# Attention and two feed-forward stages on one core: the products with v in four visits a pair instead of six, a later turn of the last rows, and weight conversions behind the exp

## The chip, the cores and the metric

One NeuronCore of a Trainium2 chip runs the whole kernel. The metric is the device time of one execution in microseconds. The kernel before took 1120.94 us in the median of three runs (1120.7 to 1121.53).

## What is computed

Rotary attention over 4 sequences of 576 positions with 8 heads of 64, then two feed-forward layers over the 2304 tokens. All is float32.

```python
def _attn_ref(q, k, v):                      # (4, 8, 576, 64)
    q_rot, k_rot = rotate(q), rotate(k)      # x1*cos - x2*sin, x1*sin + x2*cos
    scores = 1/sqrt(D) * q_rot @ k_rot.T
    attn = exp(scores - max(scores))
    attn = attn / (sum(attn) + 1e-9)
    return attn @ v
x = attention output as (2304, 512)
x = (h - tanh(h)) @ w_out,   h = x @ w_in        # 512 -> 2048 -> 512
x = (h * sigmoid(h)) @ w_out, h = x @ w_in
```

## The kernel before

The attention stage fills the first 320 us, the two feed-forward layers the rest. The program's order is written out by hand: each engine runs its instructions in the order in which the code issues them.

Attention goes by **pairs** of heads of one sequence: 16 pairs (`NP`), numbered from 0. A pair has 9 row tiles (`tiles`): 4 full tiles of 128 rows for each of the two heads, alternating, and one tile of the remaining 64 rows of both. The loop over `g` makes one **step** for each tile, 144 in all; `n` is the step within the pair, 0 to 8. Every step does this, in this order:

- `scores(g)`: TensorE multiplies a tile of q with the high and the low part of k (`kh`, `kl`) into one of two PSUM score buffers `sc`. Full precision is had by splitting numbers into a high and a low part.
- `rest(g - 2)` transposes the last columns of the p tile of two steps earlier into the score buffer of this step (steps 0, 1, 3, 5 and 7); `row_max(g)` on VectorE; `qk_low` makes low parts on VectorE; `transposes(g - 2)` turns four 128-blocks of p on TensorE (`tpp`), ScalarE copies them out to `pt`, and VectorE copies the last columns to `pr`.
- rotation of the next pair's q and k (`rope_upto`, `rope_dup` and two or one pieces from the list `rq`), on GpSimd.
- `recip_spread` (steps 4 and 7): the reciprocals of the row sums, made by GpSimd into `rw`, are turned on TensorE (`tpb`), and ScalarE copies them to `rs`.
- `pv`: products with v of the pair before. A pair has 20 (`NPV`), each two passes on TensorE, 10 into a wide half of 320 columns and then 10 into a narrow half of 256. A run of them in one step is called a **visit**; the table `PV_N` says how many there are in which step. Its index is `n2`, which is the step less 2 (modulo 9). When a half is complete, `x_out` multiplies it with `rs` on VectorE and SP stores it to `xd`.
- `conv.run`: conversions of weights for the feed-forward layers, a number of pieces by the table `CONV_RATE`. A weight tile takes four VectorE instructions, on ScalarE a Square (`wm`) and a copy (`w`), and on GpSimd a subtraction (`w`).
- `qk_high` (steps in `QK_AT`): TensorE turns the rotated q or k of the next pair (`tpq`), four blocks of 128 for q and each k, two for the remaining rows (`ar`); ScalarE copies out the high part (`qs`, `kh`, `qr`). The low part comes from `qk_low` a step later.
- `exps(g)`: exp on ScalarE into `p`. The scores of step g + 2 use the same score buffer, and its transposes need this p.

In step 2 SP issues the loads of v, in step 5 the loads of the next but one pair's q and k (`load_qk`, into `xm` and `xr`).

Of the kernel before, what the change touches and what calls it, by code (L numbers as in the profile page):

```python
# [29 lines left out]
def kernel(  # L30
# [26 lines left out]
    TW = [MAIN] * B + [B * REM]  # L57
    NH = NF // 2

    CONV_RATE = (1.6, 0.0, 0.0, 0.0, 0.0, 0.0, 0.0, 1.5, 1.5)  # L60
    RATE_0 = 0.01
    SPLIT_AT = 2

# [266 lines left out]
    TPB = 3  # L330
    NPV = 4 * (NJ + 1)
    Q0 = 256
    QK_AT = {1: 0, 3: 1, 5: 2, 6: 3}
    ON_DVE = ((1, 1),)
    R_AT = (4, 7)
    PV_N = (4, 0, 4, 2, 0, 4, 0, 4, 2)

    def attention(conv, on_rope_done, on_scores_near, on_scores_done):
        es_main, es_even, es_odd, es_rope, es_sc = (ExitStack() for _ in range(5))
# [18 lines left out]
        def load_qk(i):  # L358
            b, c = divmod(i, NPAIR)
            hs = slice(2 * c, 2 * c + 2)  # L360
            xm = [rp.tile([128, 2, NJ * D], F32, tag=f"xm{n}", name=f"xm{n}", bufs=1) for n in range(2)]
            xr = rp.tile([128, 2, D], F32, tag="xr", name="xr", bufs=1)
            for n, src in ((1, k), (0, q)):
                nc.sync.dma_start(
                    out=xm[n],
                    in_=src[b, hs, 0:MAIN, :].rearrange("h (p j) d -> p h (j d)", j=NJ),
                )
            if i == 0:
                nc.sync.dma_start(out=csr, in_=cs_rem)
            for n, src in ((0, q), (1, k)):  # L370
                nc.sync.dma_start(
                    out=xr[64 * n:64 * n + 64, :, :],
                    in_=src[b, hs, MAIN:S, :].rearrange("h p d -> p h d"),
                )
            raw_t[i] = (xm, xr)

        def load_v(i):
            b, c = divmod(i, NPAIR)
            vm = ap.tile([128, 2, NJ, D], F32, tag="vm", name="vm", bufs=2)

            vr = vr2[i % 2]
            nc.sync.dma_start(
                out=vm.rearrange("p h j d -> p h (j d)"),
                in_=v[b, 2 * c:2 * c + 2, 0:MAIN, :].rearrange("h (p j) d -> p h (j d)", j=NJ),
            )
            for h in range(2):
                nc.sync.dma_start(out=vr[64 * h:64 * h + 64, h], in_=v[b, 2 * c + h, MAIN:S, :])
            v_t[i] = (vm, vr)
# [40 lines left out]
        def rope_dup(i, u):  # L429
            if u > 0:  # L430
                a = rot_t[i][u]
                if i:
                    POOL.tensor_copy(out=a[:, :, 1, :], in_=a[:, :, 0, :])
                else:
                    ACT.activation(out=a[:, :, 1, :], in_=a[:, :, 0, :], func=ACTF.Copy)

        def qk_alloc(i):
            qk_t[i] = [qkp[i % 2].tile([128, 2 * S + (REM if nm != "qs" else 0)], F32R, tag=nm, name=nm, bufs=1)
                       for nm in ("qs", "kh", "kl")]
            qk_t[i].append(qr2[i % 2])  # L440
# [3 lines left out]
        KO = (0, 2 * S - MAIN)  # L444
        up, dn = slice(0, 64), slice(64, 128)

        def qk_high(i, u):
            src = rot_t[i][u]
            qs, kh, kl, qr = qk_t[i]
            tp = ps.tile([128, 512], F32, tag="tp", name="tpq", bufs=TPB)  # L450
            for j in range(NJ if u < 3 else 2):
                PE.transpose(tp[:, j * 128:(j + 1) * 128], src[:, j].rearrange("p e d -> p (e d)"), ident)  # L452
            if u == 0:
                parts = [(qs[up, 0:MAIN], tp[up], qs[dn, 0:MAIN]), (qs[dn, S:S + MAIN], tp[dn], qs[up, S:S + MAIN])]
            elif u < 3:
                parts = [(kh[:, KM[u - 1]], tp, kl[:, KM[u - 1]])]
            else:
                t4 = tp[:, 0:256].rearrange("p (h s) -> p h s", h=2)
                parts = [(qr[up, h, h * 64:h * 64 + 64], t4[up, h, 0:64], qr[dn, h, h * 64:h * 64 + 64])
                         for h in range(2)]  # L460
                kc = slice(MAIN, MAIN + 128)
                parts.append((kh[:, kc].rearrange("p (h s) -> p h s", h=2), t4[:, :, 64:128],
                              kl[:, kc].rearrange("p (h s) -> p h s", h=2)))
                parts.append((kh[:, 2 * S:], t4[:, 1, 64:128], kl[:, 2 * S:]))
            for hi, t, lo in parts:
                ACT.activation(out=hi, in_=t, func=ACTF.Copy)  # L466
            return parts

        def qk_low(parts):
            for hi, t, lo in parts:  # L470
                DVE.tensor_tensor(out=lo, in0=t, in1=hi.bitcast(F32), op=ALU.subtract)  # L471
# [23 lines left out]
        def row_max(g):  # L495
            st = ap.tile([128, 1], F32, tag="st", name="st", bufs=4)
            DVE.tensor_reduce(out=st, in_=s_t[g][:, :, 0:HALF], op=ALU.max, axis=AX.XY, negate=True)  # L497
            st_t[g] = st

        def exps(g):  # L500
            i, n = divmod(g, NTI)
            if n == 0:
                sum_t[i] = ap.tile([128, NTI], F32, tag="sums", name="sums", bufs=2)
            sc, st = s_t.pop(g), st_t.pop(g)
            h = tiles[n][0]
            if h != 1:
                p_t[g] = ap.tile([128, 2, S], F32, tag="p", name="p", bufs=2)
            else:
                p_t[g] = p_t[g - 1]
            p = p_t[g][:, h % 2]  # L510
            ACT.activation(out=p.rearrange("p (e s) -> p e s", e=2), in_=sc[:, :, 0:HALF],  # L511
                           func=ACTF.Exp, bias=st, accum_out=sum_t[i][:, n:n + 1])
# [111 lines left out]
        def rope_push(i):  # L624
            for n in range(5):
                rq.extend((i, n, f) for f in rope_ops(i, n, DVE if (i, n) in ON_DVE else POOL))

        def rope_upto(i, n):
            while rq and rq[0][:2] <= (i, n):
                rq.pop(0)[2]()  # L630
# [28 lines left out]
        parts = []  # L659
# [6 lines left out]
        while True:  # L666
            i, n = divmod(g, NTI)
            more = i + 1 < NP
            if 0 < i < NP and n == 2:
                load_v(i)  # L670
            if i + 2 < NP and n == 5:
                rope_upto(i + 1, 4)
                load_qk(i + 2)
                rope_push(i + 2)
            d = g - LAG - NTI
            i2, n2 = divmod(d, NTI)

            live = g < G

            if live:  # L680
                scores(g)
                if more and n == 0:
                    qk_alloc(i + 1)
                if g == 0:
                    parts.extend(first[2:5] + first[6:] + qk_high(0, 2))
            if 0 <= g - LAG < G:
                rest(g - LAG, g)
            if live:
                row_max(g)
            qk_low(parts)  # L690
            parts.clear()
            if 0 <= g - LAG < G:
                transposes(g - LAG)

            if more and QK_AT.get(n) == 0:
                rope_upto(i + 1, 1)
            elif more and n + 1 in QK_AT:
                rope_upto(i + 1, QK_AT[n + 1] + 1)
                rope_dup(i + 1, QK_AT[n + 1])
            if live:  # L700
                for _ in range(2 if n % 3 else 1):
                    if rq:
                        rq.pop(0)[2]()

            if 0 < i <= NP:
                at = R_AT if i < NP else (2, 2)
                if n == 0:
                    recips(i - 1)
                for e in (1, 0):
                    if n == at[1 - e]:  # L710
                        recip_spread(i - 1, e)
            if d >= 0:
                if n2 == 0:
                    pvq.extend((i2, m) for m in range(NPV))
                for _ in range(PV_N[n2] if live else NPV // 2):
                    if pvq:
                        pv(*pvq.pop(0))
            rate = (CONV_RATE[n] if i else RATE_0) / 2 if live else 0.0
            conv.run(rate)
            if more and n in QK_AT:  # L720
                parts.extend(qk_high(i + 1, QK_AT[n]))
            if live:
                exps(g)
            conv.run(rate)
            if g == G - NTI:
                es_rope.close()
                es_even.close()
                on_rope_done()
            if g == G - SPLIT_AT:
                on_scores_near()  # L730
            if g == G - 1:
                es_odd.close()
                es_sc.close()
                on_scores_done()
            if g >= G:
                on_tail(g - G)
            if d > 0 and i2 == NP - 1 and not pvq:
                break
            g += 1
# [234 lines left out]
    conv = Conv()  # L974
# [250 lines left out]
```

## Time and profile before

| | before |
|---|---|
| median of three runs | 1120.94 us |
| profiled execution | 1120.96 us |
| its span | 1119.2 us |
| TensorE busy | 1095.6 us (98%) |
| VectorE busy | 852.4 us (76%) |
| ScalarE busy | 681.6 us (61%) |
| GpSimd busy | 255.3 us (23%) |

The span is the time from the first to the last instruction of the program; the profiled execution's own time is 1.8 us longer. A busy TensorE isn't TensorE at its peak: matmuls are pipelined, and the ends of the records are modelled, so two records may overlap. What a piece of work costs is read from its start to the start of the next piece. GpSimd's work lies nearly all in the attention stage.

### The profile page before, as it was taken

Reading aid. Unit: us, or ns where it says so; the run is one execution under the profiler, and the core shown is the slowest. Engines: PE = TensorE matmul, PEld = TensorE weight load, DVE = VectorE, ACT = ScalarE, POOL = GpSimd, SP = SyncE. Lnnn points to the kernel's source line nnn. Section 1 sums busy time; section 2 is a strip of 40 time slices with the busy share of each in tenths; the row PEclk is TensorE's granted clock in tenths of the full one; section 3 lists DMA queues with packets and bytes.
Section 4 is the critical chain, followed back from the end, with each engine's and each line's share of the span. In section 5 each row is a group of like instructions: output and inputs, shape, how many; then the busy total and the mean of one; then the engine's idle time right before and its main releaser. Section 6 shows DMA issues by size and latency. Waiting matters only on the chain.

```text
span 1119.2 us, 17757 instructions
## 1 busy us (share of the span) xinstructions
PE 1095.6 (98%) x6304; PEld 909.0 (81%) x6304; DVE 852.4 (76%) x1536; ACT 681.6 (61%) x1447; POOL 255.3 (23%) x359
## 2 busy tenths in 40 slices
PE   5999999999999999999999999999999999999998
PEld 4777777777777889888888898888888888999997
DVE  6778778787868886889999987986646347767775
ACT  5888888887877756776767656544344335343352
POOL 6576777766410200111101000220000000000000
PEclk9999999999999999999999999999999999999999
DMA  4132323333131442344464542484524212122142
GB/s 134 48 98 87 117 69 95 96 97 95 58 114 54 159 141 76 104 141 140 155 207 146 179 161 76 133 272 138 192 104 151 85 38 76 56 95 76 34 136 76
DMA packets 85018, 126.28 MB, mean 113 GB/s; under 512 B 15552, under 2 KB 56128, under 8 KB 83136
## 3 DMA queue, kind: packets, MB, share of 16 engines
q1 hardware_dynamic: 84768, 124.88, 34.2%
q8 instruction: 50, 0.82, 0.3%
q14 instruction: 40, 0.33, 0.1%
q10 hardware_dynamic: 160, 0.26, 0.1%
HBM read 88.93 MB, written 36.18 MB: 112 GB/s over the span
## 4 chain that ended last, share of the span: by engine, by line
PE 94%; ACT 3%; DVE 2%; issue 0%; DMA 0%; SPq 0%; DVEq 0%; ACTq 0%
PE hp L788 35%; PE acc L865 26%; PE x L606 8%; PE M L949 7%; PE tpp L574 5%; PE sc L484 4%; PE sc L485 3%; PE tpq L452 2%; PE sc L491 2%; ACT p L511 1%; ACT kh L466 1%; PE acc L1093 1%; PE tpb L530 1%; PE sc L554 1%; DVE xo L960 1%
## 5 line engine op out<-in xcount | busy, mean ns | idle before, releaser
L788 PE MATMUL hp<-xh,w 128*128 128x512 f32 (+1 forms) x1280 | 388.2, 369 | 0.9 <-DVE g L1115 0.8
L788 PEld LDWEIGHTS hp<-xh,w 128*128 128x128 f32 x1280 | 234.4, 189 | 43.0 <-DVE g L1115 1.5
L788 PE MATMUL hp<-xl,w 128*128 128x512 f32 (+1 forms) x640 | 235.9, 369 | 0.0
L799 ACT ACTIVATE t<-hp 128x512 f32<-128x512 f32 (+1 forms) x120 | 66.9, 557 | 239.8 <-PE hp L788 232.9
L865 PE MATMUL acc<-gh,w 128*128 128x512 f32 (+1 forms) x640 | 193.8, 368 | 0.0
L833 DVE TENSOR_TENSOR gl<-t,gh 128x512 fp32r<-128x512 f32 (+1 forms) x120 | 77.3, 645 | 110.4 <-ACT gh L831 110.0
L497 DVE TENSOR_REDUCE st<-sc 128x1 f32<-128x576 f32 x144 | 108.8, 756 | 61.3 <-PE sc L554 35.7
L788 PEld LDWEIGHTS hp<-xl,w 128*128 128x128 f32 x640 | 120.8, 189 | 19.2
L865 PEld LDWEIGHTS acc<-gh,w 128*128 128x128 f32 x640 | 117.2, 189 | 20.4 <-issue 0.3
L254 POOL TENSOR_TENSOR w<-wf,w 128x512 fp32r<-128x512 f32 x32 | 46.3, 1458 | 371.9 <-ACT w L253 371.9
L865 PE MATMUL acc<-gl,w 128*128 128x512 f32 (+1 forms) x320 | 117.8, 368 | 0.0
L511 ACT ACTIVATE p<-sc,st 128x576 f32<-128x576 f32 x144 | 107.4, 746 | 8.3 <-DVE pr L542 4.7
L540 ACT ACTIVATE pt<-tpp 128x512 f32<-128x512 f32 x144 | 86.3, 599 | 29.3 <-PE tpp L574 28.9
L484 PE MATMUL sc<-kh,qs 128*128 128x288 f32 x256 | 85.0, 347 | 7.2 <-ACT p L511 5.2
L865 PE MATMUL acc<-w,gh 128*128 128x512 f32 x288 | 88.9, 390 | 0.0
L574 PE MATMUL tpp<-ident,p 128*128 128x128 f32 x576 | 86.7, 273 | 0.0
L484 PEld LDWEIGHTS sc<-kh,qs 128*128 128x128 f32 x256 | 49.0, 191 | 34.4 <-ACT p L511 19.0
L606 PE MATMUL x<-pt,vm 128*64 128x256 f32 (+1 forms) x512 | 75.8, 418 | 0.2 <-issue 0.2
L831 ACT ACTIVATE gh<-t 128x512 fp32r<-128x512 f32 (+1 forms) x120 | 70.6, 588 | 6.2 <-PE acc L865 6.2
L485 PE MATMUL sc<-kl,qs 128*128 128x288 f32 x256 | 73.0, 299 | 0.5 <-DVE kl L471 0.5
L949 PE MATMUL M<-w,gh 128*128 128x256 f32 x384 | 70.3, 283 | 0.0
L574 PEld LDWEIGHTS tpp<-ident,p 128*128 128x128 f32 x576 | 69.1, 141 | 0.0
(145 smaller groups left out, 2129.7 us busy)
## 6 DMA issues: line engine op xcount, KB each, us to landing
raw<-in_moe_w_in_dram SPq DMA_DIRECT2D x32, 512.0 KB, 4.0
raw<-in_moe_w_out_dram SPq DMA_DIRECT2D x28, 512.0 KB, 3.5
xin<-xd SPq DMA_DIRECT2D x14, 1024.0 KB, 5.1
wd<-wa SPq DMA_DIRECT2D x48, 256.0 KB, 2.2
wf<-wd SPq DMA_DIRECT2D x48, 256.0 KB, 3.5
pd<-xo SPq DMA_DIRECT2D x34, 256.0 KB, 2.7
xo<-pd SPq DMA_DIRECT2D x18, 256.0 KB, 5.0
xm<-in_k_dram SPq DMA_DIRECT2D x16, 256.0 KB, 2.8
```

The costliest lines, as they stand in the source:

```text
L484: PE.matmul(sc[:, e, 0:HALF], lhsT=l, rhs=kh[:, c], start=True, stop=False)
L485: PE.matmul(sc[:, e, 0:HALF], lhsT=l, rhs=kl[:, c], start=False, stop=True)
L497: DVE.tensor_reduce(out=st, in_=s_t[g][:, :, 0:HALF], op=ALU.max, axis=AX.XY, negate=True)
L511: ACT.activation(out=p.rearrange("p (e s) -> p e s", e=2), in_=sc[:, :, 0:HALF], func=ACTF.Exp, bias=st, accum_out=sum_t[i][:, n:n + 1])
L540: ACT.activation(out=dst, in_=src, func=ACTF.Copy)
L574: PE.transpose(tp[:, cc * 128:(cc + 1) * 128], p[:, p0 + cc * 128:p0 + (cc + 1) * 128], ident)
L606: PE.matmul(x[o, 0:w], lhsT=l, rhs=r, start=(cc == 0), stop=(cc == NJ))
L788: PE.matmul(hp, lhsT=w[:, a, ws], rhs=bb, start=(n == 0), stop=(n == 3 * KD - 1))
L831: ACT.activation(out=gh, in_=t, func=ACTF.Copy)
L833: DVE.tensor_tensor(out=gl, in0=t, in1=gh.bitcast(F32), op=ALU.subtract)
L865: PE.matmul(acc, lhsT=a, rhs=bb, start=(fi == 0 and n == 0), stop=(fi == NH - 1 and n == 2))
L949: PE.matmul(prod_t[name][:, tt], lhsT=al[i], rhs=bw[j], start=(first and tt == 0 and x == 0), stop=(last and tt == nt - 1 and x == 2))
```

## The change

- Products with v: `PV_N` goes from visits of 4, 4, 2, 4, 4, 2 (steps 2, 4, 5, 7, 0, 1) to visits of 6, 4, 4, 6 (steps 2, 4, 7, 0).
- The turn of the remaining rows of q and k moves from step 6 to step 7; their rotation is still completed in step 5, now at its top. The low parts of this turn follow in the same step (`LOW_NOW`).
- A turn is issued ahead of the products with v, and not at the end of the step.
- In step 5 the copy of the turned k to its high part stands behind the exp (`EXP_FIRST`).
- Weight conversions: a step's pieces come all behind the exp, and not half of them ahead of it; they stand in steps 0, 2 and 8 instead of 0, 7 and 8, at the same rates.

```diff
-    CONV_RATE = (1.6, 0.0, 0.0, 0.0, 0.0, 0.0, 0.0, 1.5, 1.5)
+    CONV_RATE = (1.6, 0.0, 1.5, 0.0, 0.0, 0.0, 0.0, 0.0, 1.5)
...
-    QK_AT = {1: 0, 3: 1, 5: 2, 6: 3}
+    QK_AT = {1: 0, 3: 1, 5: 2, 7: 3}
...
-    PV_N = (4, 0, 4, 2, 0, 4, 0, 4, 2)
+    LOW_NOW, EXP_FIRST = (7,), (5,)
+    PV_N = (6, 0, 4, 0, 0, 4, 0, 6, 0)
...
-        def qk_high(i, u):
+        def qk_high(i, u, now=True):
...
+            if now:
+                qk_evict(parts)
+            return parts
+
+        def qk_evict(parts):
             for hi, t, lo in parts:
                 ACT.activation(out=hi, in_=t, func=ACTF.Copy)
-            return parts
...
+            if more and n == 5:
+                rope_upto(i + 1, 4)
+                rope_dup(i + 1, 3)
             if i + 2 < NP and n == 5:
-                rope_upto(i + 1, 4)
                 load_qk(i + 2)
                 rope_push(i + 2)
...
-            elif more and n + 1 in QK_AT:
+            elif more and n + 1 in QK_AT and QK_AT[n + 1] < 3:
...
+            if more and n in QK_AT:
+                parts.extend(qk_high(i + 1, QK_AT[n], n not in EXP_FIRST))
             if 0 < i <= NP:
...
-            rate = (CONV_RATE[n] if i else RATE_0) / 2 if live else 0.0
-            conv.run(rate)
-            if more and n in QK_AT:
-                parts.extend(qk_high(i + 1, QK_AT[n]))
+            rate = (CONV_RATE[n] if i else RATE_0) if live else 0.0
             if live:
                 exps(g)
+            if n in EXP_FIRST:
+                qk_evict(parts)
+            if n in LOW_NOW:
+                qk_low(parts)
+                parts.clear()
             conv.run(rate)
```

TensorE, steps 4 to 7 of a middle pair, before. A step's score products are shown by their first row, and `pt` and `pr` are the turned p that the passes with v read.

```order
L606 MATMUL x<-pt_2981,vm 64x320 x4
L484 MATMUL sc<-kh,qs 128x288
L574 MATMUL tpp<-ident,p 128x128 x4
L606 MATMUL x<-pr_2982,vr_174 64x320 x2
L452 MATMUL tpq<-ident,ak 128x128 x4
L484 MATMUL sc<-kh,qs 128x288
L574 MATMUL tpp<-ident,p 128x128 x4
L452 MATMUL tpq<-ident,ar 128x128 x2
L484 MATMUL sc<-kh,qs 128x288
L554 MATMUL sc<-ident,p 128x128
L530 MATMUL tpb<-ident,rw 128x128 x2
L606 MATMUL x<-pt_2861,vm 64x256 x4
```

The same steps of the change:

```order
L611 MATMUL x<-pt_2983,vm 64x320 x2
L611 MATMUL x<-pr_2984,vr_174 64x320 x2
L489 MATMUL sc<-kh,qs 128x288
L579 MATMUL tpp<-ident,p 128x128 x4
L453 MATMUL tpq<-ident,ak 128x128 x4
L489 MATMUL sc<-kh,qs 128x288
L579 MATMUL tpp<-ident,p 128x128 x4
L489 MATMUL sc<-kh,qs 128x288
L559 MATMUL sc<-ident,p 128x128
L453 MATMUL tpq<-ident,ar 128x128 x2
L535 MATMUL tpb<-ident,rw 128x128 x2
L611 MATMUL x<-pt_2861,vm 64x256 x4
```

The wide half is complete at the end of step 4 and not in step 5, step 6 holds only scores and transposes of p, and the turn of `ar` stands in step 7.

ScalarE in the same kind of stretch, from the copy of step 5 on, before (`pt` copies the transposed p, `p,sums` is the exp):

```order
L540 ACTIVATE pt_1714<-tpp 128x4x128
L466 ACTIVATE kh<-tpq 128x512
L511 ACTIVATE p,sums<-sc,st 128x576
L540 ACTIVATE pt_1834<-tpp 128x4x128
L466 ACTIVATE qr_175<-tpq 64x64 x2
L466 ACTIVATE kh<-tpq 128x128
L466 ACTIVATE kh<-tpq 128x64
L511 ACTIVATE p,sums<-sc,st 128x576
```

And with the change:

```order
L545 ACTIVATE pt_1714<-tpp 128x4x128
L516 ACTIVATE p,sums<-sc,st 128x576
L472 ACTIVATE kh<-tpq 128x512
L545 ACTIVATE pt_1836<-tpp 128x4x128
L516 ACTIVATE p,sums<-sc,st 128x576
L545 ACTIVATE pt_1836<-tpp 128x4x128
L472 ACTIVATE qr_175<-tpq 64x64 x2
L472 ACTIVATE kh<-tpq 128x128
L472 ACTIVATE kh<-tpq 128x64
```

The exp of step 5 has changed places with the copy of k, and the four copies of the remaining rows stand in step 7, behind the exp of step 6.

SP's queue over one pair, before (`xd<-xs` stores the attention output, the 128x64 one belongs to the wide half):

```order
L618 DMA xd_75<-xs 128x256
L382 DMA vm<-in_v_dram 128x2x256
L387 DMA vr_174<-in_v_dram 64x64 x2
L364 DMA xm_2934<-in_k_dram 128x2x256
L364 DMA xm_2933<-in_q_dram 128x2x256
L371 DMA xr<-in_q_dram 64x2x64
L371 DMA xr<-in_k_dram 64x2x64
L618 DMA xd_76<-xs 128x256
L620 DMA xd_78<-xs 128x64
```

And with the change:

```order
L623 DMA xd_75<-xs 128x256
L383 DMA vm<-in_v_dram 128x2x256
L388 DMA vr_174<-in_v_dram 64x64 x2
L623 DMA xd_76<-xs 128x256
L625 DMA xd_78<-xs 128x64
L365 DMA xm_2943<-in_k_dram 128x2x256
L365 DMA xm_2942<-in_q_dram 128x2x256
L372 DMA xr<-in_q_dram 64x2x64
L372 DMA xr<-in_k_dram 64x2x64
```

The two stores of the wide half have moved ahead of the loads of q and k.

## Rows read from the trace of the kernel before

**Rows 1.** The page: shares of the chain that ended last, by engine.

```profile
PE 94%; ACT 3%; DVE 2%; issue 0%; DMA 0%; SPq 0%; DVEq 0%; ACTq 0%
```

**Rows 2.** Busy us (and instructions) of PE, PEld, DVE, ACT, POOL; clock, DMA share, GB/s.

```profile
50.00:304.00 254.00, 250.03 (x1851) 190.03 (x1848) 199.88 (x412) 208.58 (x511) 173.16 (x267) 1.00 0.30 90
```

**Rows 3.** Waits of TensorE, 50 to 304 us: total us, times, longest.

```profile
PE sc L484 <- ACT p L511: 3.7, 15, 0.4
```

**Rows 4.** Timeline (start, duration, instruction): first scores of pairs 2 and 15.

```profile
50.21 0.38 PE L484 MATMUL sc<-kh,qs 128*128 128x288 f32 x1
...
304.19 0.40 PE L484 MATMUL sc<-kh,qs 128*128 128x288 f32 x1
```

**Rows 5.** Timeline of TensorE, pair 10, steps 1 to 7; idle time in brackets.

```profile
209.71 0.60 PE L574 MATMUL tpp<-ident,p 128*128 128x128 f32 x4
...
211.24 0.38 PE L484 MATMUL sc<-kh,qs 128*128 128x288 f32 x1
...
214.37 0.60 PE L574 MATMUL tpp<-ident,p 128*128 128x128 f32 x4
...
215.16 0.38 PE L484 MATMUL sc<-kh,qs 128*128 128x288 f32 x1
...
216.69 1.30 PE L606 MATMUL x<-pt,vm 128*64 128x320 f32 x8
217.91 0.40 PE L484 MATMUL sc<-kh,qs 128*128 128x288 f32 x1
...
219.18 0.76 PE L606 MATMUL x<-pr,vr 128*64 128x320 f32 x4
219.87 0.66 PE L452 MATMUL tpq<-ident,ak 128*128 128x128 f32 x4
220.28 0.38 PE L484 MATMUL sc<-kh,qs 128*128 128x288 f32 x1
...
221.94 0.40 PE L484 MATMUL sc<-kh,qs 128*128 128x288 f32 x1 [0.23 <-ACT p L511]
```

**Rows 6.** Timeline of TensorE, pair 15: first scores of steps 5, 6, 7.

```profile
314.69 0.40 PE L484 MATMUL sc<-kh,qs 128*128 128x288 f32 x1
...
316.65 0.40 PE L484 MATMUL sc<-kh,qs 128*128 128x288 f32 x1
...
317.65 0.38 PE L484 MATMUL sc<-kh,qs 128*128 128x288 f32 x1
```

**Rows 7.** Timeline of ScalarE: exp of step 5 in pairs 10 and 15.

```profile
221.06 0.73 ACT L511 ACTIVATE p<-sc,st 128x576 f32<-128x576 f32 x1
...
316.70 0.74 ACT L511 ACTIVATE p<-sc,st 128x576 f32<-128x576 f32 x1
```

**Rows 8.** Timeline of VectorE: a weight conversion in pair 9; copy in step 5, pair 15.

```profile
187.27 1.10 DVE L154 SCALAR_TENSOR_TENSOR wa<-wm,wa 128x512 f32<-128x512 f32 x1
...
316.38 0.28 DVE L542 COPY pr<-sc 128x128 f32<-128x128 f32 x1
```

**Rows 9.** Timeline of TensorE, pair 6: first scores of step 1.

```profile
130.57 0.40 PE L484 MATMUL sc<-kh,qs 128*128 128x288 f32 x1 [0.40 <-ACT p L511]
```

**Rows 10.** Timeline of SP's queue, pair 10: a load of q, a store.

```profile
215.25 0.47 SPq L364 DMA_DIRECT2D xm<-in_q_dram  x1
...
220.59 0.34 SPq L618 DMA_DIRECT2D xd<-xs  x1
```

**Rows 11.** Timeline of GpSimd, pairs 9 and 10.

```profile
187.78 1.18 POOL L425 TENSOR_TENSOR aq<-aq,bm 128x256 f32<-128x256 f32 x1
...
209.41 0.73 POOL L520 TENSOR_TENSOR rw<-rr,own 128x128 f32<-128x128 f32 x1 [3.62 <-DVE rr L517]
...
213.71 0.39 POOL L433 COPY ak<-ak 128x256 f32<-128x256 f32 x1
...
218.36 0.74 POOL L415 TENSOR_TENSOR aq<-xm,csq 128x256 f32<-128x256 f32 x1 [0.67 <-DMA xm<-in_q_dram]
...
223.44 0.74 POOL L421 TENSOR_TENSOR bm<-xm,csk 128x256 f32<-128x256 f32 x1
```

## Prediction

> **What bounds the kernel now.** I read the chain that ended last first: TensorE holds 94% of it and no other engine over 3% [rows 1], so time is won only where TensorE does less, or waits less. The change touches the attention stage alone, so I went there next. Between 50 and 304 us TensorE is busy for 250 of 254 us, ScalarE for 209, VectorE for 200 and GpSimd for 173, at the full granted clock [rows 2]; in the list of waits ScalarE's exp is what TensorE waits for, 15 times and 3.7 us in these thirteen pairs [rows 3]. The first score product of pair 2 starts at 50.21 and that of pair 15 at 304.19 [rows 4]: a pair of heads takes 253.98/13 = 19.54 us. Everything below is a sum over one such pair, times 13, with pairs 0, 1 and 15 apart. Busy shares don't price the visits to v, though; starts do, so I took the timeline of one pair and measured from the start of one piece of work to the start of the next.
>
> **The change, part by part.**
>
> *Two visits fewer.* Step 1 now runs from its transposes of p at 209.71, through a visit of four passes with v and the turn of q, to the next scores at 211.24: 1.53 us. Step 3 does the same without a visit, 214.37 to 215.16: 0.79 us [rows 5]. The visit costs 0.74 us. What do its four passes cost inside a longer visit? Eight passes of 320 columns take 216.69 to 217.91 = 1.22, four take 219.18 to 219.87 = 0.69 [rows 5], so four more of them cost 0.53, and four of 256 columns 0.8 of that, an estimate of 0.42. So 0.74 - 0.42 = 0.32 us goes with a visit: entering it, leaving it, and the slower turn behind it. The visits of steps 1 and 5 vanish and their passes lengthen those of steps 0 and 2. I take 0.31 each, **-0.62 us a pair**; the bounds are 0.16 (only what 0.69 holds over 0.53) and 0.32.
>
> *Steps 5 to 7.* The scores of step 5 start at 217.91, those of step 7 at 221.94, behind a wait on exp [rows 5]: 4.03 us. Without the visit of step 5 (0.53 + 0.31, the 0.31 counted above) 3.19 would be left. TensorE's own work there shrinks further, since the turn of the remaining rows leaves step 6: step 5 (217.91 to 220.28 = 2.37, less 0.84) is 1.53, and step 6 without that turn is 1.00, as in pair 15, 316.65 to 317.65 [rows 5, 6]. That makes 2.53. But the scores of step 7 need the score buffer of step 5, so its exp must be over. In pair 15 nothing stands ahead of that exp but the transposed block's copy: scores at 314.69, exp at 316.70, 2.01 us later [rows 6, 7]; and exp started at 221.06, scores at 221.94 [rows 5, 7], 0.88 us more. So the change leaves 2.89 or, with the 0.08 by which VectorE starts earlier in some pairs (estimate), 2.81. I take 2.85: 3.19 - 2.85 = **-0.34 us**, bounds -0.30 and -0.66. The conversion of k, which stands ahead of this exp today, goes behind it; without that edit the wait would be longer by that conversion. The wait is shorter, not gone: VectorE's max and its copy of the transposed block now end last. The row shows exp at 316.70 just behind that copy (316.38 for 0.28) [rows 7, 8]. The Trainium skill, PSUM — Partial Sum Buffer, section on bank collisions, says that ScalarE and VectorE may not read one bank at a time, hence the order; the trace agrees, with 0.04 us between copy and exp. Were only the max awaited, some 0.2 a pair more would be won, 2.6 us in all.
>
> *The turn in step 7.* Two transposes move to a place where TensorE doesn't wait: half of the four that take 219.87 to 220.28 [rows 5], **+0.21 us**. Their four conversions now stand before the exp of step 7, which the scores of step 0 await. That exp has the long step 7 and step 8 as cover, by the pair's own order some 0.6 us more than it needs; gone, it would cost what is over. Their buffer is the one that the k of step 5 frees only when ScalarE and VectorE have read it, close to when it is wanted: 0 to 0.1, I take 0.05.
>
> *Conversions behind the exp.* In step 0 of pair 6 TensorE waited 0.40 us, at 130.57, for an exp that stood behind two weight conversions [rows 3, 9]. One wait a pair, 13 of the 15, is that of step 7, and 2 are of this kind; with what refilling costs I take **-0.12 us** a pair as a mean, bounds 0 and -0.15. On VectorE the conversions stay in the queue ahead of the next row maximum wherever they are put behind exp; step 0's are now behind the normalised output too, which waits for the last v product, and step 2's are new. There exp of step 3 has some half a microsecond in hand. I take +0.05, bounds 0 and 0.5.
>
> *The loads of q and k.* Here the change moves a queue. The output of the wide half is complete in step 4 and not 5, so SP has its two stores ahead of the loads of the next q and k, which used to be issued without regard to it: q at 215.25, 2.66 us before step 5 starts at 217.91 [rows 5, 10]. A store now follows the end of a visit by 220.59 - 219.87 = 0.72 us [rows 5, 10]. With two stores and the k load ahead, at 0.34 to 0.47 to issue [rows 10] and some 0.45 apart, q goes out 2.1 us after step 5 starts. GpSimd began its rotation 218.36 - 215.25 = 3.11 us after the issue [rows 10, 11], so it will begin at +5.2 and not +0.45. The cover is its idle time: it sat 3.62 us before 209.41 [rows 11]. Its chain from there: eight rotations, 218.36 to 223.44 and 0.74 more = 5.82; then 209.41 to 213.71 and 0.39 more = 4.69, with one weight part among them. Sum 10.5, at +15.7. TensorE wants that k in step 3 of the next pair, at my new pace at +15.5. In pairs without that weight part it comes 1.2 earlier. So the cover is used up: I take **+0.15 us** a pair, bounds 0 and 1.5 (stores at 1.2 us to issue, slower rotations).
>
> *Sum.* -0.62 - 0.34 + 0.21 + 0.05 - 0.12 + 0.05 + 0.15 = -0.62 a pair, so 18.92 us, times 13 = -8.1 us. Pair 1 loses one visit only, -0.44 (0.31 + 0.34 - 0.21); pair 0 has none, about -0.2 from the order of exp; pair 15 turns nothing and its shorter steps 5 and 6 meet the same 2.89 us, about 0. Together -8.7. The feed-forward stages keep their order, and TensorE has no idle time there for a shift to change. The profiled execution took 1120.96 us, span 1119.2, and the median is 1120.94: 1120.96 - 8.7 = **1112 us**.
>
> **Rivals.**
>
> *Nothing waits in steps 5 to 7 and nothing is late.* Then a pair loses 0.62 + 0.66 + 0.12 - 0.21 = 1.19: 15.5 + 0.7 = 16 us, 1105. Against it stands pair 15, where exp comes 2.01 us after the scores with an idle ScalarE.
>
> *Conversions in the way.* Step 2 now holds up to two VectorE conversions between the low parts of q and the maximum of step 3. If they cost 0.5 in half of the pairs, 3.3 us of the gain go: 1115.5. For it speaks VectorE's 200 of 254 us; against it, that the scores of step 5 are two steps away.
>
> *Slower: the late q and k.* The stores ahead of the loads make GpSimd's chain the longest of a pair. It decides once the turned k is over 0.15 late, eats the whole gain at about 0.8, and each further 0.1 costs 1.3 us. At 1.3 late, 1127. For it: GpSimd's chain has no slack by the sum above, and a rotation step that takes 0.74 at 218.36 took 1.18 at 187.78 [rows 11]. Against it: ten ordinary rows in a row give 15.7.
> The Trainium skill, SBUF — State Buffer, section "Who interferes with whom", has the mechanism: a VectorE instruction with two SBUF inputs and a GpSimd one that reads SBUF exclude each other for their whole length. The trace agrees with that 1.18: a VectorE conversion ran from 187.27 for 1.10 us [rows 8]; by the rule alone three such meetings in a pair's chain would add 3 x 0.44 = 1.3 us and give the time of this rival.
>
> **How the numbers follow.** Forecast 1112: 0.57. Nothing waits, 1105: 0.10. Conversions in the way, 1115.5: 0.16. Late q and k: 0.06 for a time above 1123.2, 0.06 for one that eats the gain; 0.05 for other mixes that stay faster. A measurement of this kernel can tell 0.2%, 2.2 us, from no change, so faster means under 1118.7: 0.57 + 0.10 + 0.16 + 0.05 = 0.88; within 0.06; slower 0.06. The range runs from 1106, short of the best case, to 1118, where the late loads have eaten two thirds; some 0.06 is left out below it and 0.13 above.
>
> **What would show it.** Right, if steps 1 and 5 of a middle pair take about 1.65 and 1.53 us, step 0 about 2.7, step 2 about 2.9; scores of step 5 to scores of step 7 about 2.85, still ended by exp; the first q rotation about 5 us after the scores of step 5, and the turn of k in step 3 at most some tenths late. Wrong, if the pair's length is set by a wait of that turn for GpSimd (the slower rival), if exp of step 3 or 1 ends a wait of TensorE (conversions), or if the longer visits cost more per pass than 0.13 us.

## The result, and the profile after

The changed kernel takes 1127.34 us (median of four runs, 1126.81 to 1131.1), the kernel before 1120.82 us on the same chip (1120.42 to 1121.53). The ratio is 1.0065, with a 95% interval of 1.0042 to 1.0087: **slower by 6.5 us**, where 8.7 us less were forecast. The profiled execution took 1126.97 us, its span is 1125.1, at a granted clock of 1.00.

The first place to look is the page's chain that ended last, by engine and then by line. Before, TensorE held 94% of it [rows 1]. After:

```profile
PE 78%; POOL 10%; DVE 3%; ACT 3%; DMA 3%; issue 1%; SPq 1%; POOLq 0%; DVEq 0%; ACTq 0%
PE hp L799 35%; PE acc L876 26%; PE M L960 7%; PE x L611 3%; DMA xm<-in_q_dram 3%; POOL bm L422 2%; PE tpp L579 2%; POOL ak L416 2%; ACT p L516 1%; PE sc L489 1%; POOL aq L416 1%; POOL w L169 1%; POOL aq L426 1%; PE tpq L453 1%; PE sc L490 1%
```

GpSimd (POOL) has 10% of the chain and DMA 3%, by way of the load of q. Neither had more than a trace of it before. The busy times of the attention stage, in the same stretch and columns as [rows 2], say that TensorE idles:

```profile
50.00:304.00 254.00, 238.31 (x1799) 186.56 (x1798) 207.55 (x401) 202.37 (x496) 189.43 (x272) 1.00 0.30 88
```

TensorE is busy for 238 of 254 us and no longer for 250. GpSimd's busy time went up from 173 to 189 us, with five instructions more. The first scores of pairs 2 and 15, as in [rows 4]:

```profile
49.40 0.38 PE L489 MATMUL sc<-kh,qs 128*128 128x288 f32 x1
...
309.97 0.38 PE L489 MATMUL sc<-kh,qs 128*128 128x288 f32 x1
```

A pair takes 260.57/13 = 20.04 us and not 19.54, nor the 18.92 of the forecast. Thirteen times 20.04 - 18.92 = 1.12 us is 14.6 us, and 1112 + 14.6 = 1126.6: nearly the whole miss lies in these pairs. Where in a pair? I took the first scores of each step to the first scores of the next, as a mean over the thirteen pairs (us):

| step | 0 | 1 | 2 | 3 | 4 | 5 | 6 | 7 | 8 | pair |
|---|---|---|---|---|---|---|---|---|---|---|
| before | 2.35 | 2.38 | 2.41 | 1.54 | 2.76 | 2.37 | 1.65 | 2.51 | 1.57 | 19.54 |
| changed | 2.70 | 1.76 | 3.03 | **2.66** | 2.82 | 1.54 | 1.30 | 2.73 | 1.52 | 20.04 |
| changed, pair 2 alone | 2.71 | 1.65 | 2.91 | 1.55 | 2.76 | 1.53 | 1.28 | 2.74 | 1.51 | 18.63 |

In pair 2 TensorE has no wait long enough to be listed, and it takes 18.63 us. On the average, step 3 takes 1.1 us more than there, and steps 1, 2 and 4 together 0.3 us. Step 3 has the turn of the first head's k (`ak`). The waits of TensorE from 50 to 304 us (total us, times, longest), where [rows 3] has the wait for exp:

```profile
PE tpq L453 <- POOL ak L434: 12.1, 10, 1.7
PE sc L489 <- ACT p L516: 2.1, 5, 0.7
PE tpq L453 <- POOL aq L426: 0.4, 2, 0.3
```

The waits for exp are fewer, 2.1 us against 3.7, but they have moved: before, 13 of 15 stood at the scores of step 7, and now four of five stand at the scores of steps 3 and 5, which need the exp of steps 1 and 3. New are 12.1 us in which TensorE waits at L453 for GpSimd's copy of the rotated k, in ten places. And GpSimd itself, over the same stretch, waits for the load of q:

```profile
POOL aq L416 <- DMA xm<-in_q_dram: 59.7, 12, 6.2
```

So GpSimd idles for 59.7 us and then hurries, with TensorE behind it. One pair shows the whole chain: pair 9 to pair 10, its step 5 first. The first scores of step 5 on TensorE, then SP's queue:

```profile
200.18 0.40 PE L489 MATMUL sc<-kh,qs 128*128 128x288 f32 x1
...
201.06 0.33 SPq L623 DMA_DIRECT2D xd<-xs  x1
201.45 0.43 SPq L625 DMA_DIRECT2D xd<-xs  x1
201.97 0.41 SPq L365 DMA_DIRECT2D xm<-in_k_dram  x1
202.43 1.57 SPq L365 DMA_DIRECT2D xm<-in_q_dram  x1
```

The two stores wait for the visit of step 4 and for VectorE's product; k and q are issued behind them, q 2.25 us after step 5 began, where the kernel before issued it 2.66 us ahead of step 5 [rows 5, 10]. GpSimd's chain from there (start, duration; idle time in brackets), and TensorE's turn at its end:

```profile
206.62 0.73 POOL L416 TENSOR_TENSOR aq<-xm,csq 128x256 f32<-128x256 f32 x1 [4.88 <-DMA xm<-in_q_dram]
...
209.14 0.92 POOL L416 TENSOR_TENSOR aq<-xm,csq 128x256 f32<-128x256 f32 x1
...
211.53 1.19 POOL L416 TENSOR_TENSOR ak<-xm,csk 128x256 f32<-128x256 f32 x1
212.68 1.18 POOL L422 TENSOR_TENSOR bm<-xm,csk 128x256 f32<-128x256 f32 x1
...
214.73 1.28 POOL L169 TENSOR_TENSOR w<-wa,w 128x512 fp32r<-128x512 f32 x1
215.97 0.73 POOL L426 TENSOR_TENSOR ak<-ak,bm 128x256 f32<-128x256 f32 x1
216.66 1.17 POOL L416 TENSOR_TENSOR ak<-xm,csk 128x256 f32<-128x256 f32 x1
217.78 0.39 POOL L434 COPY ak<-ak 128x256 f32<-128x256 f32 x1
...
218.22 0.66 PE L453 MATMUL tpq<-ident,ak 128*128 128x128 f32 x4 [1.65 <-POOL ak L434]
```

The rotations begin 6.44 us after step 5, GpSimd runs without a gap from there, and the copy of k ends 17.99 us after step 5 began. TensorE has stood idle for 1.65 us. From here on I call the forecast's late loads **theory L**: stores that wait, then loads, then GpSimd's chain, are the whole of the loss. Its rivals: **C**, conversions on VectorE in the way of an exp; and the longer visits costing more than was thought.

### The profile page after: what moved, and what is told of

Read it like the earlier page. It is cut to its first block, busy times and chain, and to the rows that moved or that the text cites. A ratio compares the mean times of both kernels' runs of the same rounds, so it can differ in the third digit from the quotient of the medians.

```text
span 1125.1 us, 17799 instructions
## 1 busy us (share of the span) xinstructions
PE 1089.6 (97%) x6304; PEld 911.5 (81%) x6304; DVE 864.9 (77%) x1536; ACT 680.0 (60%) x1447; POOL 268.7 (24%) x359
## 4 chain that ended last, share of the span: by engine, by line
PE 78%; POOL 10%; DVE 3%; ACT 3%; DMA 3%; issue 1%; SPq 1%; POOLq 0%; DVEq 0%; ACTq 0%
PE hp L799 35%; PE acc L876 26%; PE M L960 7%; PE x L611 3%; DMA xm<-in_q_dram 3%; POOL bm L422 2%; PE tpp L579 2%; POOL ak L416 2%; ACT p L516 1%; PE sc L489 1%; POOL aq L416 1%; POOL w L169 1%; POOL aq L426 1%; PE tpq L453 1%; PE sc L490 1%
```

## Experiments

Each ratio is to the kernel before on the same chip (1121.85 us for e1 to e4, 1121.22 for e5 to e8, 1121.58 for e9 to e11; 1120.82 beside the changed kernel). So times of different groups compare to about 1 us, and the ratio and the pair are the better measure. "Pair" is the mean of the thirteen middle pairs.

### e1: the two stores behind the loads

The changed kernel, with the wide half's stores kept back until step 5 has issued the loads of q and k.

```diff
 def x_out(i, x, rs, e, hold=False):
...
+    if e and hold:
+        held.append(stores)
+    else:
+        stores()
...
     if i + 2 < NP and n == 5:
         load_qk(i + 2)
         rope_push(i + 2)
+    if n == 5 or g >= G:
+        while held:
+            held.pop(0)()
```

> The changed kernel with one thing undone: the two stores of the wide half are issued in step 5, behind the loads of the next q and k, and not in step 4 ahead of them. All engines but SP keep the order of the changed kernel. Theory L (the late q and k: the stores stand ahead of the loads in SP's queue, GpSimd starts its rotations some 6 us later and the turn of k in step 3 waits for it): 1108 to 1111 us, 18.6 to 18.8 us a pair, no wait of TensorE for GpSimd. Rival C (the conversions in step 2 and behind the exp hold VectorE and GpSimd): little moves, 1122 to 1128 us.

Measured: **1111.14 us**, ratio 0.9906 (0.9891 to 0.9921), pair 18.79. SP's queue in pair 9, whose step 5 starts at 193.38, and GpSimd's first rotation:

```profile
188.34 0.39 SPq L365 DMA_DIRECT2D xm<-in_k_dram  x1
188.78 0.46 SPq L365 DMA_DIRECT2D xm<-in_q_dram  x1
...
192.85 0.73 POOL L416 TENSOR_TENSOR aq<-xm,csq 128x256 f32<-128x256 f32 x1
...
194.14 0.34 SPq L627 DMA_DIRECT2D xd<-xs  x1
```

q goes out 4.60 us ahead of step 5 and the rotation starts 0.53 us ahead of it, behind other work of GpSimd and not behind a load. TensorE's only listed waits from 50 to 304 us are for exp, in pairs 3, 6, 12 and 13:

```profile
PE sc L489 <- ACT p L516: 2.1, 7, 0.4
```

The order of two stores and two loads on one queue is worth some 16 us of the changed kernel's 1127 (20.04 - 18.79 = 1.25 us a pair, times 13). Taken together, the rest of the change does what it was forecast to do: 1112 was the forecast, with 0.15 us a pair for late loads in it. Without that term it says 1110; 1111.14 is measured, where the kernel before took 0.9 us more than in the forecast.

### e2: late loads alone, in the kernel before

The kernel before, with the loads of q and k in step 6, behind the stores. `rope_push`, which queues their rotations for GpSimd, stands with the loads and moves along.

```diff
                 rope_upto(i + 1, 4)
+            if i + 2 < NP and n == 6:
                 load_qk(i + 2)
                 rope_push(i + 2)
```

> The kernel before with the one step of theory L alone: the loads of the next but one pair's q and k are issued in step 6 and not in step 5, so that SP has the two stores of the wide half ahead of them, as in the change. Visits, turns, exp and conversions stay as before. Theory L: GpSimd's first rotation begins some 7 us later, the turn of k in step 3 waits 0.8 to 1.9 us a pair, 1130 to 1145 us. Rival C: 1119 to 1123 us, as the kernel before.

Measured: 1152.77 us, 1.0269 (1.0253 to 1.0285), pair 21.69. The direction is L's, the size is above the range and the place is another: from 50 to 326 us it is the turn of q in step 1 (2.4 to 5.1 us there, 2.38 before) that waits.

```profile
PE tpq L452 <- POOL aq L425: 19.0, 12, 2.6
```

q is issued 4.0 us after step 5's scores in most pairs, and GpSimd begins 7.2 to 8.3 us after them. That is 1.9 us later than in the changed kernel on the average (7.61 against 5.70), so the dose was larger than the change's, and q's six rotations then end too late for step 1, two steps before k's are due. That late loads alone can cost more than the change does is shown; the price of the change's own delay isn't measured by this run.

### e3 and e9: the conversions back in their old places

e3 is the changed kernel with the rates of before; e9 is e1 with them.

```diff
-CONV_RATE = (1.6, 0.0, 1.5, 0.0, 0.0, 0.0, 0.0, 0.0, 1.5)
+CONV_RATE = (1.6, 0.0, 0.0, 0.0, 0.0, 0.0, 0.0, 1.5, 1.5)
```

> The changed kernel with the table of the weight conversions as before (steps 0, 7 and 8 and not 0, 2 and 8), still behind the exp. Theory L: the loads stay behind the stores, 1123 to 1128 us. Rival C: the loss goes, 1112 to 1118 us.

> The changed kernel with the wide half's stores held until load_qk has issued its loads (as in e1), and with the old places of the conversions (steps 0, 7, 8 instead of 0, 2, 8). It asks what the conversions' place is worth once the loads are not late. Theory L (all of the loss is late loads; the conversions' place is worth the -0.12 us a pair of the prediction, 13 pairs, 1.6 us): 1111.1 + 1.6 = 1112.7, so 1111.5-1114. Rival (the conversions in step 7 stand ahead of the exp that step 8 or step 0 waits for, as the waits of before name it, and the 6 us between the changed kernel and the one with old places hold by themselves): 1116-1119, with waits of the scores for ScalarE's exp above 5 us in all.

Measured: e3 1133.32 us, 1.0104 (1.0089 to 1.0119), pair 20.33; e9 1111.53 us, 0.991 (0.9894 to 0.9927). Rival C falls as far as step 2 goes: with the conversions out of it the kernel gets slower still. But L as I stated it for e3 misses by 5 us, and the trace says why. TensorE's waits of e3:

```profile
PE sc L489 <- ACT p L516: 5.9, 13, 1.2
PE tpq L453 <- POOL aq L426: 5.5, 6, 2.0
PE tpq L453 <- POOL ak L434: 2.9, 4, 1.2
```

GpSimd's part of a weight conversion (L169, 1.27 us and more) now falls among the first eight rotations in nine of the thirteen pairs, in the changed kernel in five. So the turn of q is late too. From the first rotation to the copy of k GpSimd needs 11.39 us on the average and not 10.97. With the loads on time, the place of the conversions is worth nothing that can be told (e9 against e1: ratios of 0.991 and 0.9906, and 18.79 us a pair in both). The new places gain only while GpSimd is the late one.

### e4: the new visits alone

The kernel before with the visits of the change; turn, order of exp and conversions stay.

```diff
-    PV_N = (4, 0, 4, 2, 0, 4, 0, 4, 2)
+    PV_N = (6, 0, 4, 0, 0, 4, 0, 6, 0)
```

> The kernel before with the new table of visits alone (6, 4, 4, 6), which completes the wide half in step 4; turns, exp and conversions as before. Theory L: this edit alone puts the stores ahead of the loads, 1124 to 1132 us, with the turn of k in step 3 waiting for GpSimd. Rival C: two visits fewer are won and nothing is lost, 1111 to 1116 us.

Measured: 1132.32 us, 1.0094 (1.0077 to 1.011), pair 20.33, just above the range. The visits alone bring the loss: they complete the wide half in step 4 and so put the stores ahead of the loads. They wait for GpSimd in the same two turns:

```profile
PE sc L484 <- ACT p L511: 7.1, 19, 1.1
PE tpq L452 <- POOL ak L433: 5.7, 7, 1.2
PE tpq L452 <- POOL aq L425: 4.8, 4, 1.8
```

Scores of step 5 to scores of step 7 take 3.24 us here, and 2.84 in the changed kernel on the average, where exp goes ahead of k's conversion and the small turn has left step 6: 0.4 us a pair for these two edits.

### e7: no weight conversions

The changed kernel with no weight conversions during attention; they run later, so only the attention stage is read, in one profile.

```diff
-    CONV_RATE = (1.6, 0.0, 1.5, 0.0, 0.0, 0.0, 0.0, 0.0, 1.5)
-    RATE_0 = 0.01
+    CONV_RATE = (0.0,) * 9
+    RATE_0 = 0.0
```

> The changed kernel without weight conversions during attention (they all come at the start of the feed-forward stage, so only the attention part is to be read, the whole time is longer by their cost). The stores stay ahead of the loads. It asks why the turned k was 1 to 2 us late where the prediction had 0.15: if it is VectorE's conversions that lengthen GpSimd's eight rotations from 5.8 to 7 or 8 us, these return to 5.8 and the wait in step 3 goes, with 18.6 to 18.8 us a pair; if it is the late start of the rotations by itself, a wait of 0.5 us or more stays in most pairs.

Measured: pair **18.62**, no wait of TensorE from 50 to 304 us, although the stores stand ahead of the loads as in the changed kernel and GpSimd idles for 5.9 to 7.6 us a pair before the first rotation. GpSimd, pair 9 to 10:

```profile
198.50 0.73 POOL L416 TENSOR_TENSOR aq<-xm,csq 128x256 f32<-128x256 f32 x1 [7.55 <-DMA xm<-in_q_dram]
199.19 0.73 POOL L422 TENSOR_TENSOR bm<-xm,csq 128x256 f32<-128x256 f32 x1
...
203.55 0.73 POOL L422 TENSOR_TENSOR bm<-xm,csk 128x256 f32<-128x256 f32 x1
...
206.52 0.39 POOL L434 COPY ak<-ak 128x256 f32<-128x256 f32 x1
```

Every rotation takes 0.73 us and the chain 8.41 us (198.50 to 206.91); in the changed kernel it takes 10.97 on the average. The rotations begin 5.58 us after step 5 on the average, as late as in the changed kernel (5.70), so the late start alone is covered: the chain ends at +14.0, and TensorE wants that k at +15.5 by the forecast's count. Nor do the conversions alone make the wait, since e1 and e9 have them, with the loads on time. It takes both: the start, and the 2.5 us a pair that the conversions add to the chain. So L as I stated it, the late loads as the whole of the loss, isn't right: C, as it was put on record for e1, named GpSimd too, and that part of it is needed. No run parts the 2.5 us further; by the trace of the changed kernel GpSimd's own part of the conversions (L169) has 1.06 of them, the first eight rotations have 1.0, and the rest lies behind those. Who slows the rotations? VectorE in the changed kernel, beside the rotations of 209.14, 211.53 and 212.68 that took 0.92, 1.19 and 1.18 us:

```profile
208.52 0.96 DVE L144 TENSOR_SCALAR wa<-raw 128x512 int32<-128x512 int32 x1
...
211.25 0.87 DVE L147 SCALAR_TENSOR_TENSOR wa<-raw,wa 128x512 int32<-128x512 int32 x1
212.16 1.11 DVE L151 SCALAR_TENSOR_TENSOR wa<-raw,wa 128x512 int32<-128x512 int32 x1
```

The last two are conversions with two inputs. Of the 152 rotations of this size from 50 to 304 us, 65 overlap such a conversion and take 1.17 us in the median, up to 1.27; the other 87 take 0.73 in the median. The Trainium skill, SBUF — State Buffer, section "Who interferes with whom", says that such an instruction and a GpSimd one that reads SBUF exclude each other for their whole length, while a VectorE instruction with at most one SBUF input, outside the two-port modes, lets GpSimd pass. For two inputs these rows, and 0.73 throughout in e7, agree. For one input they don't settle it: four of the 87 take 0.90 to 0.93 us, the one of 209.14 among them, and those run into L144, a conversion with one input; whether it ran in a two-port mode no run here shows, though its 0.42 us in the median of the kernel before, against 0.69 for the two-input ones of the same size, would fit that.

### e8: q loaded ahead of k

```diff
-            for n, src in ((1, k), (0, q)):
+            for n, src in ((0, q), (1, k)) if i else ((1, k), (0, q)):
```

> The changed kernel with the load of q ahead of that of k (from pair 1 on; the rotations begin with q). The load of q goes out 0.45 us earlier, behind the same two stores. Theory L, with GpSimd's chain as the bound in most pairs: 0.45 us a pair less where it waits, 1121 to 1124 us. Rival C: no change from the changed kernel, 1126 to 1129 us.

Measured: 1119.26 us, 0.9986 (0.9976 to 0.9995), pair 19.48. The first rotation begins 4.99 us after step 5's scores on the average, and 5.70 in the changed kernel: 0.71 earlier, and the pair is 0.56 shorter. It gained 8 us where I expected 3 to 6, since the start moved by more than the 0.45 us that I had counted on: q is issued 0.33 us earlier and is in use 0.39 us sooner after that. The wait for k is a fifth of what it was, while the waits for exp rise from 2.1 to 5.2 us:

```profile
PE sc L489 <- ACT p L516: 5.2, 13, 1.0
PE tpq L453 <- POOL ak L434: 2.3, 4, 1.0
```

### e5, e6, e10, e11: the visit of step 4 in step 5

A second way to have the stores behind the loads: the wide half completes in step 5. e5 is the changed kernel with that alone; e6 adds the exp of step 3 ahead of k's conversion; e10 and e11 are e5 with the conversions of step 2 in step 5, or back in step 7.

```diff
-    PV_N = (6, 0, 4, 0, 0, 4, 0, 6, 0)
+    PV_N = (6, 0, 0, 4, 0, 4, 0, 6, 0)
# e6 also
-    LOW_NOW, EXP_FIRST = (7,), (5,)
+    LOW_NOW, EXP_FIRST = (7,), (3, 5)
# e10 instead of that
+    CONV_RATE = (1.6, 0.0, 0.0, 0.0, 0.0, 1.5, 0.0, 0.0, 1.5)
# e11 instead of that
+    CONV_RATE = (1.6, 0.0, 0.0, 0.0, 0.0, 0.0, 0.0, 1.5, 1.5)
```

> The changed kernel with the second visit in step 5 and not in step 4 (visits of 6, 4, 4, 6 in steps 2, 5, 7, 0): the wide half is complete in step 5, so that SP has its stores behind the loads again, without a held store. Theory L: no wait for GpSimd in step 3. Step 5 now covers its own exp, so scores of step 5 to scores of step 7 follow TensorE's work; step 4 is short, and exp of step 3 stands behind the copy of k, so scores of step 3 to scores of step 5 take 3.24 us (measured between steps 5 and 7 with that order in e4) where TensorE's work is 3.0. 18.55 us a pair, 1107 to 1110 us. Rival C: 1122 us or more.

> As e5, with the copy of k behind the exp in step 3 too. Theory L: scores of step 3 to scores of step 5 fall from 3.24 to TensorE's work of 3.0, 18.3 us a pair, 1104 to 1107 us. Rival C: 1122 us or more.

Measured: e5 1117.95 us, 0.9971 (0.996 to 0.9982), pair 19.32; e6 1121.75, 1.0005 (0.9995 to 1.0014). No wait for GpSimd in either, as L says, but both miss their ranges. In e5 step 4, without a visit, takes 2.35 us on the average (1.79 to 3.20) and not 1.7, which is what is left of e5's 3.24 for steps 3 and 4. In pair 10 (VectorE, ScalarE, TensorE):

```profile
212.32 0.81 DVE L154 SCALAR_TENSOR_TENSOR wa<-wm,wa 128x512 f32<-128x512 f32 x1
213.16 0.76 DVE L502 TENSOR_REDUCE st<-sc 128x1 f32<-128x576 f32 x1
213.84 0.28 DVE L547 COPY pr<-sc 128x128 f32<-128x128 f32 x1
...
214.15 0.74 ACT L516 ACTIVATE p<-sc,st 128x576 f32<-128x576 f32 x1 [0.40 <-DVE pr L547]
...
215.04 0.40 PE L489 MATMUL sc<-kh,qs 128*128 128x288 f32 x1 [0.62 <-ACT p L516]
```

A conversion of step 2 stands ahead of the row maximum of step 3, whose exp is late, and step 5's scores wait for its buffer. This is rival C, in a place where no visit covers it. e6 moves ScalarE's order, and its step 4 stays at 2.35: that order wasn't the late one. Its step 5 got longer by 0.29 us. The reading was then put to two runs:

> The kernel e5 (visit in step 5 instead of step 4, so that the stores stand behind the loads) with the conversions of step 2 moved to step 5. In e5's trace the conversion L154 of step 2 (0.81 us at 212.32) stands ahead of the row max and the copy of step 3, the exp of step 3 waits for that copy, and step 4, which has no visit there, waits for that exp (2.35 us a step instead of 1.55). Theory V (that order on VectorE is the whole of e5's miss): step 4 falls to 1.55-1.7, the pair to 18.5-18.7, the time to 1117.95 - 13 x 0.7 = 1109, so 1106-1111. Rival (step 4 without a visit is too short for ScalarE's own work, whatever VectorE does, or the conversions only take the wait to step 6 or 7): 1114-1119.

> The kernel e5 with the conversions back in steps 0, 7, 8. Theory V: step 4 falls to 1.55-1.7 as in e10, and the conversions in step 7 cost what e9 shows for them (0 to 2 us over the kernel): 1108-1113. Rival (step 4 is ScalarE's own): step 4 stays at 2.2-2.4 and the time at 1116-1120.

Measured: e11 **1111.49 us**, 0.9909 (0.9894 to 0.9924), with step 4 at 1.70 us in every pair; e10 1121.68 us, 1.0002 (0.9993 to 1.0012), with step 4 at 1.70 too, but step 7 at 2.7 to 4.4 us. e11 settles that step 4 isn't ScalarE's own. In e10 the wait only moved to step 7, as the rival there said, but at a higher price than its 1114 to 1119. TensorE's waits of e10, and VectorE and TensorE in steps 6 and 7 of pair 11:

```profile
PE tpb L535 <- DVE kl L476: 7.4, 7, 1.5
...
240.81 1.23 DVE L154 SCALAR_TENSOR_TENSOR wa<-wm,wa 128x512 f32<-128x512 f32 x1
241.97 0.95 DVE L144 TENSOR_SCALAR wa<-raw 128x512 int32<-128x512 int32 x1
...
243.50 0.68 DVE L476 TENSOR_TENSOR kl<-tpq,kh 128x512 fp32r<-128x512 f32 x1
...
244.23 0.44 PE L535 MATMUL tpb<-ident,rw 128*128 128x128 f32 x2 [1.50 <-DVE kl L476]
```

Two conversions stand ahead of the low part of step 5's k, and the transposes of the reciprocals at L535 need the buffer that this low part frees. e1, e9 and e11 are the best of the kernels here, 10 us under the kernel before, and can't be told apart.

## Why the prediction was wrong

The sign was wrong by one term, the loads of q and k. Point by point, with pair 2 as the undisturbed pair:

- **Two visits fewer, -0.62.** Right. Steps 1, 5, 0 and 2 were to take 1.65, 1.53, 2.7 and 2.9 us; undisturbed they take 1.65, 1.53, 2.71 and 2.91.
- **Steps 5 to 7, -0.34.** Right: 2.81 us (1.53 + 1.28) against 2.85, and still ended by exp, though TensorE's idle time of 0.07 us there is too short for the list of waits. The exp of step 5 and the scores of step 7 in pair 9 are 0.88 us apart, as forecast:

```profile
202.11 0.74 ACT L516 ACTIVATE p<-sc,st 128x576 f32<-128x576 f32 x1
...
202.99 0.40 PE L489 MATMUL sc<-kh,qs 128*128 128x288 f32 x1
```

- **The turn in step 7, +0.21 and +0.05.** Right: that step went from 2.51 to 2.73, and nothing waits for its buffer.
- **Conversions behind the exp, -0.12 and +0.05.** Before, the mean pair of 19.54 was 0.13 over its undisturbed 19.41, in the main by long steps 0 and 8, and those are gone in e1: the first is right. The second is some 0.16 in e1, whose pair is 18.79 and not 18.63: at the scores of step 3 or 5, exp of step 1 or 3 now ends four waits, though exp of step 3 was to have half a microsecond in hand. Together the two terms come to about nothing. The old places cost as much in e9.
- **The loads of q and k, +0.15, bounds 0 and 1.5.** This is the step that failed. The queue was read rightly: q was forecast to go out 2.1 us after step 5 starts, and goes out 2.06 to 2.68 after it. The cover that I named, GpSimd's idle time, was rightly said to be used up. But the end of the chain, +15.7 against a wanted +15.5, was a sum of undisturbed rotations and one weight part. The measured means are a start at +5.70 and not +5.2, since the load takes longer from its issue to GpSimd's first rotation than the one row of 3.11 us (3.2 to 3.7 in most pairs, 3.9 and 4.2 in pairs 2 and 9), and a chain of 10.97 and not 10.5, since the rotations run beside VectorE's conversions (the first eight take 6.84 us in sum, and 5.86 in e7). That is +16.67, 1.17 late, and step 3 is 1.1 us longer. The term is some 1.1 us a pair, 14 us in all. The undisturbed pair is 18.63, where the forecast without this term says 18.77; step 3 adds 1.11 and steps 1, 2 and 4 add 0.29, which makes the measured 20.04 to 0.01.

The slower rival, "the late q and k", had the mechanism, the place (the turn of k in step 3), the point from which it decides and the time, 1127. I gave it 0.12 in all. Its time was in part luck: of its 1.3 us late, put down to three slow rotations, 1.17 were measured, and 0.5 of that is the later start of the rotations. The argument against it, ten ordinary rows in a row, took a rotation of 0.74 us for ordinary, though [rows 11] showed one of 1.18 us beside a conversion. A chain that I had found to have no slack counts its errors on one side only: in three pairs the chain has no weight part and is some 1.2 us shorter, which gains nothing once TensorE doesn't wait, while what the queue and the conversions added was paid in full. So the middle value of the term lay well above what the sum of ordinary rows gave.

Rival C isn't what made the changed kernel slow (e3), but its late exps cost some 0.16 us a pair in e1, and e5 and e10 show that it is larger one step away.

## What to carry to other kernels

Where an edit makes a result complete earlier or later, look at what is queued behind its store: on a queue that issues in order, a store that waits for an engine holds back every load behind it, and here two stores ahead of two loads cost 16 us while GpSimd idled. Ask too what else lies in the chain behind those loads: here the late start was free without the conversions (e7), and the conversions were nearly free with an early start (e1). Put prefetches ahead of stores that have to wait. And where a sum says that a chain just fits, price it with the slow rows of the trace as well as the quick ones, since a chain without slack can only come out late.

## What the runs showed of the hardware

- The same rotation on GpSimd takes 0.73 us in e7 and, in the changed kernel, up to 1.27 us beside a VectorE conversion with two inputs; beside one with a single input it took 0.90 to 0.93 us four times. With GpSimd's own part of the conversions, that adds 2.5 us to a chain of 8.4. I had known of the slow row and not how much of a pair it would touch.
- Issuing a load isn't a constant: the load of q held SP's queue for 0.46 us in most pairs, and for 1.57 us in the pair shown, where the rotation began 6.44 us after step 5 and not some 5.4. It isn't the conversions alone, since e7 has such issues too (1.35 and 1.72 us in pairs 2 and 9); what made it longer wasn't tried.
